# A list-scheduled attention stage, DMA transposes and a new prologue in a fused attention + token-MLP kernel

## The chip, the cores and the metric

One core of one Trainium2 chip. The metric is the device time of one execution in microseconds; the profile's span is 1 to 3 us shorter than the timed execution. TensorE does the matmuls; VectorE and ScalarE copy its results out of PSUM (the memory that matmuls write, used here as 8 banks) and do elementwise work; GpSimd does the causal masks and small operations; and SyncE issues every DMA. The program gives each engine its own list of instructions, in an order that is fixed when it is built. The kernel after was timed twice, in rounds of its own; the experiments ran in later rounds, in which the kernel before took 743.85 to 744.43 us (743.42 in the first). So a difference of under about 2 us between the kernel after and an experiment is not clear of noise, and small effects are read from the stages of the trace instead (one profiled execution each).

## The reference, cut to what matters

```python
xn = layernorm(A_x[0])                       # 2048 tokens x 1024
A: q,k,v = xn@wq, xn@wk, xn@wv               # 32 heads of 32, 4 segments of 512 tokens
   per segment: p = softmax(q k^T/sqrt(32) + causal mask);  a_dot = p v
                a_mem = phi(q) M / (phi(q) z);  o = g*a_mem + (1-g)*a_dot
                M += phi(k)^T v;  z += sum phi(k)          # phi(t) = t>0 ? t+1 : exp(t)
   a = o @ wo
B: h = layernorm(xn); u = gelu(h^T w1 + b1)  # over tokens: 2048 -> 3584 -> 2048
   y = u w2 + b2
out = A_x + a + y^T
```

`h` is the layer norm of a layer norm, so both kernels get it from one set of statistics of x.

## The kernel before

A chunk is 128 tokens (16 chunks), a unit is four heads of one segment (32 units). The kernel has four stages: prologue (loads, statistics, first hidden columns), hidden layer (896 matmuls of 128x128x512), attention with the second MLP layer between its pieces, and a tail for the last attention unit.

Prologue: statistics of a pair of chunks on VectorE, `h` on GpSimd, transposes of xn on TensorE, then six matmuls of the hidden layer per chunk:

```python
for p in range(n_pair + 2):
    if p < n_pair:
        self.ln_stats(2 * p); self.ln_stats(2 * p + 1); self.ln_small(2 * p)
    if 1 <= p <= n_pair:
        self.ln_bias(2 * p - 2)
        for c in (2 * p - 2, 2 * p - 1): self.ln_apply(c)     # xn on ACT or DVE, h on GpSimd
    # [cut]
    if p >= 2:
        for c in (2 * p - 4, 2 * p - 3):
            self.x_transpose(c)          # 8 TensorE transposes, ScalarE copies out of PSUM
            self.early_hidden(c)
```

Attention: a fixed order per unit of four heads, with fixed numbers of MLP matmuls (`main_emit`) between its pieces:

```python
self.logits(u, 0)
if u: self.combine(u - 1)
self.main_emit(n0)
self.logits(u, 1); self.main_emit(n1)
self.logits(u, 2); self.main_emit(n2)
self.weigh(u, 0); self.weigh(u, 1)
# [cut] proj_q of u+2, then
self.o_transpose(u - 1, 2)               # 4 TensorE transposes + ScalarE copy
self.k_transpose(u + 1, 3)               # 4 TensorE transposes + phi out of PSUM
self.weigh(u, 2)                         # [cut] proj_k
self.weigh(u, 3)                         # [cut] proj_v
self.main_emit(n3)
```

The softmax here doesn't subtract the row's maximum and nothing guards it: scores larger than these inputs give would overflow.

## Time and profile before

743.42 us, median of 2 runs (742.68 to 744.17). From the timeline of TensorE (start of the first hidden matmul, of the first v projection, end of the last matmul, span):

| stage | from | to | us |
|---|---|---|---|
| before the first hidden matmul | 0 | 18.9 | 18.9 |
| hidden layer | 18.9 | 223.6 | 204.7 |
| attention and output | 223.6 | 736.4 | 512.8 |
| after the last matmul | 736.4 | 742.3 | 5.9 |

Two lines of the page: the span, and busy time by engine.

```profile
span 742.3 us, 11641 instructions
...
PE 707.3 (95%) x5058; PEld 342.0 (46%) x5154; DVE 277.1 (37%) x617; ACT 280.4 (38%) x301; POOL 112.5 (15%) x154
```

The chain of waits, a part of the hidden layer: start, us, what. A piece starts every 10.79 us and holds 50 matmuls, 215.8 ns each; 49 of them are recorded, as the record of one is missing from the trace.

```profile
60.61 10.74 PE ps_all L188 x49
71.41 10.74 PE ps_all L188 x49
```

The timeline of GpSimd in the prologue gives its pace:

```profile
19.89 2.65 POOL L609 TENSOR_SCALAR h<-xin,ln_rs,ln_nb 128x1024 bf16<-128x1024 bf16 x2 [0.59 <-DVE ln_nb L594]
24.25 2.65 POOL L609 TENSOR_SCALAR h<-xin,ln_rs,ln_nb 128x1024 bf16<-128x1024 bf16 x2 [1.71 <-DVE ln_nb L594]
28.60 2.65 POOL L609 TENSOR_SCALAR h<-xin,ln_rs,ln_nb 128x1024 bf16<-128x1024 bf16 x2 [1.70 <-DVE ln_nb L594]
```

A pair of chunks of `h` comes every 4.36 us, and GpSimd waits each time for VectorE. TensorE needs 12 x 0.216 + 16 x 0.055 = 3.5 us for the same pair.

The tail, from the timeline: eight additions in four rows, each followed by its store.

```profile
732.98 3.41 PE L188 MATMUL ps_all<-wo_sb,xnT_68 128*128 128x512 bf16 x15 [0.69 <-ACT xnT_68 L835]
734.92 1.29 DVE L966 TENSOR_TENSOR fin_8027<-ps_all,fin_8027 128x512 bf16<-128x512 f32 x2 [10.19 <-PE ps_all L188]
...
738.52 1.27 DVE L966 TENSOR_TENSOR fin_8030<-ps_all,fin_8030 128x512 bf16<-128x512 f32 x2
...
739.82 0.33 SPq L210 DMA_DIRECT2D out_dram<-fin_8030  x1
```

### The profile page before, as it was taken

The numbers are of one execution on the slowest core, as the hardware profiler recorded it, in microseconds if no ns is written. First come the engines' busy times: TensorE is split into PE (matmuls) and PEld (weight loads), VectorE is DVE, ScalarE is ACT, GpSimd is POOL, SyncE is SP. The second block draws the span as 40 slices with busy tenths as digits, with TensorE's granted clock in tenths as the row PEclk, the third lists the DMA queues.
The fourth block names the chain that finished last, engine by engine and source line by source line (L and its number), as shares of the span: only waits on it lengthen the run. The fifth ranks groups of instructions, "written<-read, shape, count | busy, mean of one in ns | idle before, by whom it ended". The sixth has DMA issues, their size and how long they took to land.

```text
span 742.3 us, 11641 instructions
## 1 busy us (share of the span) xinstructions
PE 707.3 (95%) x5058; PEld 342.0 (46%) x5154; DVE 277.1 (37%) x617; ACT 280.4 (38%) x301; POOL 112.5 (15%) x154
## 2 busy tenths in 40 slices
PE   0999999999999999999999999999999999999996
PEld 0444444444444454454444455444455444444452
DVE  6930000000002234335454555554545554444543
ACT  2682121211212443544444343344444344443540
POOL 3640000000000221221121211121211112211220
PEclk9999999999999999999999999999999999999999
DMA  9429322323508141641615415052451606425003
GB/s 253 145 83 218 97 57 82 88 57 91 97 1 223 29 107 29 136 103 34 135 38 100 103 34 135 1 136 55 81 108 29 135 16 120 89 47 108 15 13 115
DMA packets 164603, 65.77 MB, mean 89 GB/s; under 512 B 125642, under 2 KB 156362, under 8 KB 164554
## 3 DMA queue, kind: packets, MB, share of 16 engines
q1 hardware_dynamic: 164554, 65.04, 37.5%
q8 instruction: 40, 0.66, 0.4%
q14 instruction: 9, 0.07, 0.0%
HBM read 59.79 MB, written 5.24 MB: 88 GB/s over the span
## 4 chain that ended last, share of the span: by engine, by line
PE 91%; DVE 4%; issue 1%; SPq 1%; ACT 1%; DMA 1%; POOL 0%; POOLq 0%; DVEq 0%
PE ps_all L188 89%; PE ps_all L194 2%; DVE ln_st L575 1%; SPq L210 1%; DVE ln_st L574 1%; DMA brow_51<-in_B_b_dram 1%; ACT pT L743 0%; DVE ln_mv L576 0%; POOL pT L749 0%; DVE xn_tmp_76 L607 0%; DVE ln_rs L584 0%; DVE fin_8030 L966 0%; DVE fin_8029 L966 0%; ACT xn_tmp_75 L604 0%; DVE xn_tmp_74 L607 0%
## 5 line engine op out<-in xcount | busy, mean ns | idle before, releaser
L743 ACT ACTIVATE pT<-ps_all 128x1536 bf16<-128x1536 f32 (+1 forms) x96 | 152.9, 1593 | 192.9 <-PE ps_all L188 192.9
L749 POOL TENSOR_SCALAR_AFFINE_SELECT pT<-pT 128x512 bf16<-128x512 bf16 x128 | 87.0, 692 | 585.1 <-ACT pT L743 585.1
L662 ACT ACTIVATE gT<-ps_all,b1c 128x512 bf16<-128x512 f32 x56 | 37.8, 689 | 134.5 <-PE ps_all L188 134.5
L710 DVE CAST vA_63<-ps_all 128x512 bf16<-128x512 f32 x16 | 11.1, 694 | 187.9 <-PE ps_all L188 187.7
L188 PE MATMUL ps_all<-h,w1s_79 128*128 128x512 bf16 x311 | 72.0, 382 | 2.7 <-issue 2.2
L188 PE MATMUL ps_all<-h,w1s_80 128*128 128x512 bf16 x314 | 72.3, 381 | 0.3
L188 PE MATMUL ps_all<-h,w1s_81 128*128 128x512 bf16 x251 | 55.6, 379 | 0.3
L188 PE MATMUL ps_all<-gT,w2h_663 128*128 128x512 bf16 x213 | 52.9, 380 | 1.1 <-issue 0.8
L188 PE MATMUL ps_all<-gT,w2h_662 128*128 128x512 bf16 x219 | 53.6, 381 | 0.3
L188 PE MATMUL ps_all<-gT,w2h_665 128*128 128x512 bf16 x214 | 53.0, 380 | 0.9 <-issue 0.6
L188 PE MATMUL ps_all<-gT,w2h_664 128*128 128x512 bf16 x218 | 53.3, 381 | 0.4 <-issue 0.2
L783 DVE CAST ost_1683<-ps_all 128x264 bf16<-128x264 f32 (+1 forms) x64 | 23.7, 391 | 71.8 <-PE ps_all L188 71.8
L783 DVE CAST ost_1684<-ps_all 128x264 bf16<-128x264 f32 (+1 forms) x64 | 23.7, 391 | 68.2 <-PE ps_all L188 68.1
L188 PEld LDWEIGHTS ps_all<-h,w1s_80 128*128 128x128 bf16 x320 | 31.4, 98 | 38.1 <-issue 0.6
L188 PEld LDWEIGHTS ps_all<-h,w1s_79 128*128 128x128 bf16 x320 | 30.7, 98 | 36.8 <-issue 3.0
L188 PEld LDWEIGHTS ps_all<-h,w1s_81 128*128 128x128 bf16 x256 | 25.0, 98 | 30.2
L188 PE MATMUL ps_all<-wo_sb,oT_1691 128*128 128x512 bf16 x126 | 32.4, 379 | 0.2
L188 PEld LDWEIGHTS ps_all<-gT,w2h_665 128*128 128x128 bf16 x224 | 20.6, 98 | 25.2 <-issue 2.5
L188 PEld LDWEIGHTS ps_all<-gT,w2h_663 128*128 128x128 bf16 x224 | 20.6, 98 | 25.2 <-issue 2.5
L188 PE MATMUL ps_all<-wo_sb,xnT_68 128*128 128x512 bf16 x127 | 30.5, 379 | 0.7 <-ACT xnT_68 L835 0.7
L188 PEld LDWEIGHTS ps_all<-gT,w2h_662 128*128 128x128 bf16 x224 | 19.3, 98 | 25.3 <-issue 6.4
L188 PEld LDWEIGHTS ps_all<-gT,w2h_664 128*128 128x128 bf16 x224 | 19.3, 98 | 25.3 <-issue 6.4
(167 smaller groups left out, 870.0 us busy)
## 6 DMA issues: line engine op xcount, KB each, us to landing
w1s_79<-in_B_w_dram SPq DMA_DIRECT2D x5, 1024.0 KB, 5.4
w1s_80<-in_B_w_dram SPq DMA_DIRECT2D x5, 1024.0 KB, 6.0
w1s_81<-in_B_w_dram SPq DMA_DIRECT2D x4, 1024.0 KB, 5.8
wq_658<-in_A_wq_dram SPq DMA_DIRECT2D x16, 256.0 KB, 3.0
wq_659<-in_A_wq_dram SPq DMA_DIRECT2D x16, 256.0 KB, 6.9
wk_660<-in_A_wk_dram SPq DMA_DIRECT2D x16, 256.0 KB, 2.9
wk_661<-in_A_wk_dram SPq DMA_DIRECT2D x16, 256.0 KB, 4.8
w2h_662<-in_B_w_dram SPq DMA_DIRECT2D x8, 448.0 KB, 4.9
```

The costliest lines, as they stand in the source:

```text
L188: ins = self.nc.tensor.matmul(*args, **kwargs)
L194: ins = self.nc.tensor.transpose(out, in_, ident)
L210: ins = es.eng.dma_start(out_ap, in_ap)
L574: fw.op("dve", lambda e: e.bn_stats(st[:, 0:6], src[:, 0:512]), reads=[self.R_xin[c]], writes=[R])
L575: fw.op("dve", lambda e: e.bn_stats(st[:, 6:12], src[:, 512:1024]), reads=[self.R_xin[c], R], writes=[R])
L662: fw.op("act", lambda e: e.activation(self.gT[:, fc, half * 512:(half + 1) * 512], self.bank(b), ACT.Gelu_apprx_tanh, bias=self.b1c[:, fc: ...
L710: fw.op("dve", lambda e: e.tensor_copy(self.vA[i][:, c, :, 0:D_HEAD], self.bank(b).rearrange("p (h d) -> p h d", d=D_HEAD)), reads=[self.R ...
L743: fw.op("act", lambda e: e.activation(self.pT[:, :, off:off + total], self.ps[:, 0:4, 0:total], ACT.Exp, scale=SCALE), reads=self.R_bank[0:4],
L749: fw.op("pool", lambda e: e.affine_select(d, d, pattern=[[0, 4], [1, P]], compare_op=ALU.is_ge, fill=0.0, base=0, channel_multiplier=-1), ...
L783: fw.op("dve", lambda e: e.tensor_copy(dst, self.ps[:, b, 0:n * VW]), reads=[self.R_bank[b]], writes=[self.R_ost[o][qb]])
```

## The change

Its intent: keep TensorE on dense matmuls from about 7 us to the end. Dense work (2816 matmuls of 512 columns) stays the same. The filler is what may be put anywhere between attention's tasks: the matmuls of the second MLP layer and of the output projection. The diff is about 1,500 lines; its core, with cuts marked:

```diff
 # --- scheduler: every operation carries an assumed duration, the builder keeps a clock per engine
+class _Flow:                       # [cut]
+    def run(self, goal, total):
+        while self.crit:           # attention's TensorE tasks, in program order
+            now = fw.now["pe"]
+            nxt = self.advance(now)          # emit ACT/DVE/POOL/SP work that is ready by now
+            # [cut] pick the first of the next 5 tasks whose inputs and PSUM banks are ready
+            ahead = fill.done >= goal * (1 - len(self.crit) / n_crit)
+            if pick is not None and (ahead or not fill.can(now)) and not (...):
+                self.emit_pe(pick); continue
+            if fill.can(now):
+                fill.step(); continue         # one dense MLP matmul
+            # [cut] else wait
+    GOAL = 1060                      # of 1088 filler matmuls
 # --- transposes: 352 on TensorE become 72 DMA transposes
-            for j in range(N_DCH):
-                fw.tp(bb[:, j * P:(j + 1) * P], src[:, j * P:(j + 1) * P], self.ident[:])
+        self.fw.dma(self.xnT[s][:, :, cc * P:(cc + 1) * P], self.xn_tmp[c % 4][:],
+                    reads=[self.R_xnt[c % 4]], writes=[self.R_xnT[c]], transpose=True)
+            # the same for k (24 of 128 KB) and o (32 of 128 KB)
 # --- logits: three windows per two units, one 512-column exponential per PSUM bank
-        fw.op("act", lambda e: e.activation(self.pT[:, :, off:off + total], self.ps[:, 0:4, 0:total], ACT.Exp, ...))
+        box = fl.pe(mms, reads, banks=len(slots), wall=True, ns=637)
 # --- prologue: x and w1 loaded by rows in turn, statistics shared with ScalarE, h on VectorE
+        self.load_x(0, 1); self.load_x(1, 1); self.load_w1(0, 1)   # [cut] x2 w1.1 x3 w1.2-3 x4-5 w1.4-5
+        fw.dma(self.brow[0:N_FCH, :], ..., reads=[self.R_brow], writes=[self.R_brow])
+        fw.dma(self.brow[32:32 + N_TCH, :], ..., reads=[], writes=[self.R_brow])
+        # [cut] x6-7 w1.6-7 ... x14-15 w1.14-15
+        self.stats(0); self.stats(1); self.ln_h(0, 0); self.ln_h(0, 1); self.stats(3)
+        for c in range(N_TCH):
+            self.early_hidden(c)                       # 8 matmuls
+            if c % 2 == 0:
+                self.stats(c + 5)                      # odd: 2 ScalarE passes, 3 GpSimd operations
+                self.stats(c + 2, 0)                   # even: VectorE, 2 GpSimd operations
+                self.ln_h(c + 1)
+                self.stats(c + 2, 1)
+                self.ln_h(c + 2)
+            if c == 10:
+                self.bias_columns()                    # 8 VectorE transposes of the bias rows
 # --- tail: stores by half, the last one by quarter
+                fw.op("dve", ..., reads=[self.R_bank[b], R_fin[i][h]], writes=[R_fin[i][h]])
+                fw.dma(self.out_d[:, 4 * s + i, h * 512 + c0:h * 512 + c1], dst, reads=[R_fin[i][h]],
+                       writes=[self.R_out[4 * s + i]], is_output=True)
```

## The prediction

> **What bounds the kernel now.** TensorE. The page gives it 95% busy; the chain of waits is 91% TensorE; the granted clock is 1.00. Dense stretches of the chain move 50 matmuls in 10.79 us, 215.8 ns each, as the Trainium skill has it ("TensorE: Matmul & The Clock Gate", Back-to-back issue gap: N/2.4 + 2.5). The 742 us, from the timeline of TensorE:
>
> - 0 to 18.8 us: no useful matmul. First x lands at 3.45; statistics wait for a 5.5 us DMA issue; TensorE sits 15.0 us on a bias row.
> - 18.8 to 225.7: hidden layer. 896 matmuls x 215.8 ns = 193.4 us, 128 transposes x 55 ns = 7.0 us, about 6.5 us of cold clock and waits.
> - 225.7 to 736.4: attention and output, 510.7 us. 1920 dense matmuls = 414.3; 1280 33-column matmuls at 25.5 ns = 32.6; 192 of 132 columns at 57 ns = 11; logits about 0.95 us x 32 = 30.5; 224 transposes x 55 ns = 12.3. Sum 501; the other 10 us are bubbles.
> - 736.4 to 742.3: eight vector additions of 0.65 us in a row, then a 2 us store.
>
> **What the change does.** The 2816 dense matmuls stay.
> - All 352 TensorE transposes go: 19.3 us of TensorE, all on the critical path. They become DMA transposes (16 of 256 KB in the hidden stage, 56 of 128 KB later). Trainium skill, "DMA: Bandwidth & Descriptors", DMA Transpose (X-bar): they run beside ordinary DMAs; no run here shows their cost. DMA is 37% busy, so I expect them hidden.
> - Prologue: loads of x and w1 interleaved by rows, half the statistics on ScalarE, h on VectorE, 14 warming matmuls, bias transposes off TensorE. Chain: x at 3.45, two statistics 1.4, aggregation 0.2, two small GpSimd operations about 0.7, half of h 0.3, hops: first hidden matmul at 6 to 8 us instead of 18.8. VectorE needs about 2.7 to 3.4 us per pair of chunks against 3.45 of TensorE: 2 to 4 us of bubbles.
> - Hidden layer ends near 7 + 193.4 + 3.5 = 204 us.
> - Attention: 488.5 us of TensorE work is left (501 less 12.3); logits in three windows per two units cost about the same. ScalarE works more (320 exponentials of about 0.6 us instead of 96 of 1.59 us, 190 us against 153) but stays half busy, VectorE too; the filler hides their latency. Bubbles 4 us (was 10): 492 us, ending at 696.
> - Tail: stores by half, last one by quarter: 3.5 us instead of 5.9.
>
> Profile span about 699.5; the times run about 1 us over the span: **701 us**, 8 in 10 between 692 and 716. Chances: faster by over 2% 0.97, within 2% 0.025, slower 0.005. In parts: prologue and its bubbles 14, x transposes 7, other transposes 12, bubbles 6, tail 2.5.
>
> **What the profile would show.** First h matmul before 8 us at 216 ns spacing; attention's first matmul at 202 to 206; no transposes on TensorE; TensorE 96 to 97% busy; attention 489 to 497 us long; DMA transposes landing in 2 to 5 us; ScalarE near 300 us busy in all; last 3 to 4 us without matmuls.
>
> **What would make it wrong.** DMA transposes that take the one issuing queue long (several us each) would delay w2 and wq loads behind them; TensorE would then wait for DMA in attention, 10 to 20 us in all. A build-time order whose assumed durations are off would stall in-order queues at the logits windows, which need six or seven free banks. A statistics chain slower than 1.73 us per chunk would stretch the early hidden stage.

## More of the kernel before

Busy time by stretch: stretch, its length, busy us (and instructions) of PE, PEld, DVE, ACT and POOL, granted clock, DMA share, GB/s.

```profile
0.00:10.00 10.00, 0.00 (x0) 0.00 (x0) 4.70 (x11) 3.00 (x4) 0.70 (x6) 1.00 0.77 186
10.00:20.00 10.00, 2.50 (x13) 1.40 (x14) 8.28 (x30) 1.56 (x4) 6.47 (x7) 1.00 1.11 340
20.00:30.00 10.00, 9.95 (x73) 5.63 (x72) 9.41 (x25) 7.72 (x10) 6.59 (x5) 1.00 0.70 211
30.00:50.00 20.00, 17.19 (x135) 9.77 (x137) 12.58 (x34) 15.29 (x19) 11.71 (x10) 1.00 0.01 2
```

TensorE does next to nothing for 18.9 us. VectorE is the busiest engine from 10 to 20 us, and from 20 to 30 us it is nearly as full as TensorE.

A small framework tracks every buffer as a `Res` with its last writer and its readers, and emits semaphore waits from that.

```python
def _waits(self, es, reads, writes, extra=()):
    # [cut] add(t): wait for token t; [cut] the rules for PSUM banks
    for r in reads:
        add(r.w)
    for r in writes:
        w = r.w
        if w is not None and isinstance(w.key, tuple) and w.key[0] == "dma" and r.r:
            pass
        else:
            add(w)                      # a second write waits for the first one
        for t in r.r.values():
            add(t)                      # and for every reader
```

## The result, and the profile after

713.83 us, median of 2 runs (713.44 to 714.21). The ratio to the kernel before is 0.9601, 95% interval 0.9573 to 0.9628. A ratio is the mean time of one kernel's fast runs over that of the other's of the same rounds, so it is not quite the ratio of the medians quoted. The prediction was 701, with 692 to 716 as its range: inside the range, and 12.8 us too low.

| stage (us) | before | after | change | predicted after |
|---|---|---|---|---|
| before the first hidden matmul | 18.9 | 6.9 | -12.0 | 7 |
| hidden layer | 204.7 | 201.6 | -3.1 | 197 |
| attention and output | 512.8 | 496.7 | -16.1 | 492 |
| after the last matmul | 5.9 | 6.6 | +0.7 | 3.5 |
| span | 742.3 | 711.7 | -30.6 | 699.5 |

The three misses are each 3 to 5 us. (The prediction put the hidden layer's end of before at 225.7; it is 223.57. I had taken the start of the view's own stretch for the start of the stage. That moved 2 us between two rows of its own account of before, and not its time for after.)

The page after:

```profile
span 711.7 us, 11510 instructions
...
PE 684.6 (96%) x4733; PEld 329.5 (46%) x4822; DVE 266.0 (37%) x600; ACT 281.6 (40%) x513; POOL 119.0 (17%) x236
```

TensorE's busy share went from 95% to 96% while the time fell by 4%, and the weight loads stayed at 46%. The Trainium skill ("Trainium Kernel Development and Optimization", Performance Expectations) calls matmul busy time a bad metric for how close a kernel is to the roofline; this agrees. The same passage calls the busy share of weight loads a good one; that did not show the gain here either, since the transposes took their weight loads with them (5154 recorded before, 4822 after).

The same stretches after:

```profile
0.00:10.00 10.00, 8.46 (x29) 3.32 (x30) 4.55 (x10) 6.21 (x11) 3.01 (x14) 1.00 0.75 236
10.00:20.00 10.00, 5.68 (x20) 2.10 (x18) 3.49 (x8) 6.93 (x13) 4.41 (x13) 0.83 0.78 271
20.00:30.00 10.00, 9.95 (x47) 4.51 (x47) 6.65 (x16) 6.41 (x12) 5.95 (x16) 1.00 0.69 229
30.00:50.00 20.00, 18.21 (x83) 7.92 (x83) 12.72 (x30) 5.65 (x10) 12.07 (x20) 1.00 0.32 97
```

From 10 to 20 us TensorE is busy for only 5.68 us, at a mean clock of 0.83, and VectorE for only 3.49 us. The timelines of TensorE, VectorE and GpSimd in that stretch (start, us, engine, what, idle before and who ended it), then of SyncE's queue:

```profile
6.85 3.61 PE L217 MATMUL ps_all<-h,w1all 128*128 128x512 bf16 x16 [0.28 <-DVE h L810]
14.78 2.59 PE L217 MATMUL ps_all<-h,w1all 128*128 128x512 bf16 x8 [4.32 <-DVE h L810]
```

```profile
8.80 0.21 DVE L798 BATCH_NORM_AGGREGATE ln_mv<-ln_st 128x2 f32<-128x12 f32 x1
14.09 0.55 DVE L810 TENSOR_SCALAR h<-xin,ln_mv,ln_r 128x1024 bf16<-128x1024 bf16 x1 [5.08 <-POOL ln_r L802]
```

```profile
9.81 0.56 POOL L789 TENSOR_TENSOR ln_r<-ln_t,mhalf 128x1 f32<-128x1 f32 x1
11.12 0.30 POOL L785 TENSOR_SCALAR ln_t<-ln_mv 128x1 f32<-128x1 f32 x1 [0.75 <-ACT xn_tmp L781]
12.28 0.19 POOL L787 TENSOR_TENSOR ln_t<-ln_t 128x1 f32<-128x1 f32 x1 [0.86 <-ACT xn_tmp L783]
12.55 0.56 POOL L789 TENSOR_TENSOR ln_r<-ln_t,mhalf 128x1 f32<-128x1 f32 x1
13.10 0.23 POOL L800 TENSOR_SCALAR ln_t<-ln_mv 128x1 f32<-128x1 f32 x1
```

```profile
5.11 5.89 SPq L245 DMA_DIRECT2D brow<-in_B_b_dram  x2
11.05 0.42 SPq L245 DMA_DIRECT2D xin<-in_A_x_dram  x1
```

Read together: chunk 2's variance is ready on VectorE at 9.0 us, but GpSimd makes its reciprocal root (L800, L802) only at 13.1, after it has done chunk 3's and chunk 5's three operations (L785 to L789). Chunk 5's wait for its load and for ScalarE. TensorE sits from 10.3 to 14.8. On SyncE, the two tiny bias rows hold the queue for 5.9 us, and no x is asked for meanwhile.

The clock then drops: the record has one window of 3.4 us at half clock from 15.8 us. The Trainium skill ("TensorE: Matmul & The Clock Gate", What's actually happening) says that an idle window of about 3.4 us brings the clock down to half. This trace agrees in the half clock and in the 3.4 us, but the 3.4 us before the drop were not idle: TensorE had been back at work for 1.0 us.

The tail, from the chain of waits after, and the end of the timeline:

```profile
702.72 0.70 DVE fin L1223
...
703.54 1.80 DMA out_dram<-fin
...
705.78 1.79 DMA out_dram<-fin
...
707.63 1.53 DMA out_dram<-fin
...
709.25 0.42 DVE fin L1223
```

Stores wait for stores in a row, and the last addition waits for a store.

The DMA transposes, from the page's list of issues (KB are not given for transposes; the last number is the median us to landing):

```profile
pk<-pkT SPq DMA_TRANSPOSE x24, 2.3
...
xnT<-xn_tmp SPq DMA_TRANSPOSE x16, 3.4
oT<-o_s SPq DMA_TRANSPOSE x16, 2.4
```

### The profile page after: what moved, and what is told of

Same layout as the page of the kernel before. It is cut to its first block, busy times and chain, and to the rows that moved or that the text cites. A ratio compares the mean times of both kernels' runs of the same rounds, so it can differ in the third digit from the quotient of the medians.

```text
span 711.7 us, 11510 instructions
## 1 busy us (share of the span) xinstructions
PE 684.6 (96%) x4733; PEld 329.5 (46%) x4822; DVE 266.0 (37%) x600; ACT 281.6 (40%) x513; POOL 119.0 (17%) x236
## 4 chain that ended last, share of the span: by engine, by line
PE 90%; DVE 3%; DMA 3%; issue 1%; ACT 1%; POOL 1%; SPq 0%; DVEq 0%
PE ps_all L217 90%; DMA xin<-in_A_x_dram 1%; DMA brow<-in_B_b_dram 1%; DVE h L810 1%; DMA w2h<-in_B_w_dram 1%; DMA out_dram<-fin 1%; DVE stg L1309 1%; DVE ln_st L796 1%; DVE ln_st L794 1%; POOL ln_r L802 0%; ACT pT L1044 0%; SPq L245 0%; DVE bt L832 0%; POOL ln_t L800 0%; DVE pkT L935 0%
## 5 line engine op out<-in xcount | busy, mean ns | idle before, releaser
L217 PE MATMUL ps_all<-gT,w2h 128*128 128x512 bf16 x850 | 219.5, 379 | 6.1 <-DVE stg L1309 2.2
L1044 ACT ACTIVATE pT<-ps_all 128x512 bf16<-128x512 f32 x320 | 162.0, 619 | 127.0 <-PE ps_all L217 127.0
L217 PE MATMUL ps_all<-h,w1all 128*128 128x512 bf16 x878 | 194.8, 381 | 7.2 <-DVE h L810 6.3
L1052 POOL TENSOR_SCALAR_AFFINE_SELECT pT<-pT 128x256 bf16<-128x256 bf16 (+3 forms) x176 | 93.5, 538 | 545.7 <-ACT pT L1044 542.0
L217 PEld LDWEIGHTS ps_all<-h,w1all 128*128 128x128 bf16 x896 | 87.7, 98 | 114.3 <-issue 9.0
L217 PEld LDWEIGHTS ps_all<-gT,w2h 128*128 128x128 bf16 x896 | 79.6, 97 | 85.3 <-issue 9.9
L217 PE MATMUL ps_all<-xnT,wq 128*128 128x512 bf16 x253 | 59.8, 379 | 2.3 <-ACT pT L1044 1.8
L217 PE MATMUL ps_all<-xnT,wk 128*128 128x512 bf16 x253 | 60.3, 379 | 0.2
L217 PE MATMUL ps_all<-wv_sb,xnT 128*128 128x512 bf16 x248 | 59.9, 379 | 0.4
L217 PE MATMUL ps_all<-vA,pT 128*128 128x33 bf16 x1280 | 51.6, 178 | 0.4
L948 ACT ACTIVATE vA<-ps_all 128x512 bf16<-128x512 f32 x18 | 10.8, 599 | 83.5 <-PE ps_all L217 83.5
```

Source lines behind the costliest of these rows:

```text
L217: ins = self.nc.tensor.matmul(out, *args, **kwargs)
L948: self.flow.op({"act": (lambda e, b: e.activation(dst, view(self.bank(b)), ACT.Copy), 635, 560), "dve": (lambda e, b: e.tensor_copy(dst, v ...
L1044: fl.op({"act": (lambda e, b, slot=slot: e.activation(pT[:, slot, :], self.bank(b), ACT.Exp, scale=SCALE), 620, 530)}, [], [R[slot]], box= ...
L1052: fl.op({"pool": (lambda e, ap=ap, pat=pat: e.affine_select(ap, ap, pattern=pat, compare_op=ALU.is_ge, fill=0.0, base=0, channel_multiplie ...
```

## The experiments

Eleven kernels were run. All gave correct results. Stage ends are read from the timeline as in the tables above.

### The two halves of the attention stage's change: before_dmat and after_pet

*before_dmat* is the kernel before with all 352 transposes made DMA transposes, with its order, prologue and tail kept (and with 110 DMA semaphores instead of 64):

```diff
 def x_transpose(self, c):
-    # 8 TensorE transposes, then a ScalarE copy
+    self.fw.dma(self.xnT[s][:, :, cc*P:(cc+1)*P], self.xn_tmp[c % 4][:], ..., transpose=True)
 def k_transpose(self, u, b):
-    # 4 TensorE transposes of kT, exp and phi from PSUM
+    # exp and phi of kT in SBUF, then
+    fw.dma(self.pk[j][:], self.etmp[1][:], ..., transpose=True)
 def o_transpose(self, u, b):
-    # 4 TensorE transposes, then a ScalarE copy
+    self.fw.dma(self.oT[s % 2][:, g, :]..., self.o_s[o][:]..., transpose=True)
```

> The kernel before with its 352 TensorE transposes made DMA transposes, nothing else (static order, old prologue, old tail). Theory A (the transposes' 19.3 us of TensorE time are wholly on the critical path, and the static order hides the DMA's 2.5 to 3.5 us as well as the list scheduler does): 722 to 726 us, attention stage 497 to 500 us. Rival B (the list scheduler is what hides the transposes' latency and the attention stage's waits): 730 us or more, with new TensorE waits on DMA.

*after_pet* is the changed kernel with the transposes of k and o put back on TensorE, as tasks of the scheduler:

```diff
-            self.flow.dma(lambda: self.fw.dma(self.pk[u % 3][:], self.pkT[:], ..., transpose=True), ...)
+            self.pe_transpose(self.pkT, self.R_pkT, pk, ...)   # 4 transposes, copy on ACT or DVE
-        t = self.flow.dma(lambda: self.fw.dma(oT[:, g, :]..., os[:]..., transpose=True), ...)
+        t = self.pe_transpose(os, R_os, oT[:, g, :], ...)
```

> The changed kernel with the 224 transposes of k and o back on TensorE, as tasks of the scheduler (evacuated by ScalarE or VectorE as it chooses); the 128 of x stay DMA transposes. Theory A (they cost TensorE 12.3 us on the critical path): 725 to 729 us, attention stage 506 to 511 us against 495 now. Rival B (the filler hides them or frees of DMA waits give half back): 718 us or less.

| | median time (4 runs if not said) | ratio to before (95%) | attention stage |
|---|---|---|---|
| before | 744.43 (7 runs) | 1 | 512.8 |
| before_dmat | 729.03 | 0.9798 (0.9781 to 0.9814) | 498.5 |
| after | 713.83 (2 runs, other rounds) | 0.9601 | 496.7 |
| after_pet | 730.88 | 0.9817 (0.9802 to 0.9831) | 513.5 |

With the old order, the DMA transposes shorten the attention stage by 14.3 us. With the scheduler, taking the k and o transposes back costs 16.8. In this stage, then, the DMA transposes are worth 14 to 17 us, and the scheduler with its new windows is worth 1.8 (498.5 against 496.7), or nothing where transposes are on TensorE (512.8 against 513.5). Even the 1.8 is not clear of noise: pool_order below has the same attention order and took 498.6. TensorE time alone would be 224 x 55 ns = 12.3 us, so after_pet lies above theory A's numbers (730.88 us, stage 513.5). Of the 2.0 us on top in before_dmat, 1.7 is the wait of TensorE in front of the first logits, which is gone. For the 4.5 us on top in after_pet no cause is shown: TensorE waits 3.6 us in front of transposes there, but less elsewhere.

As a whole before_dmat met neither of its theories' numbers (729 against 722 to 726, or 730 and more): its attention stage is as theory A had it, but its hidden stage got only 1.2 us shorter, not 7. The waits of TensorE in it, longest first, say why:

```profile
PE ps_all L194 <- DMA brow<-in_B_b_dram: 14.9, 1, 14.9
PE ps_all L188 <- POOL h L609: 5.9, 3, 2.8
```

Without the transposes TensorE waits for `h` instead. Most of the 7 us were not on the critical path of the old prologue. About 1 us more went to the DMA transposes themselves: VectorE had to wait until one had freed its buffer, and the next pair of `h` came 5.34 us after the pair before (24.34 to 29.68) instead of 4.36:

```profile
24.96 0.86 DVE L607 TENSOR_SCALAR xn_tmp<-xin,ln_rs,ln_nb 128x1024 bf16<-128x1024 bf16 x1 [0.72 <-DMA xnT<-xn_tmp]
...
29.68 2.65 POOL L609 TENSOR_SCALAR h<-xin,ln_rs,ln_nb 128x1024 bf16<-128x1024 bf16 x2 [2.80 <-DVE ln_nb L594]
```

### The tail: tail_own

```diff
-        R_fin = [[Res(...) for h in range(2)] for i in range(4)]
+        R_fin = [[Res(...) for h in range(2 + (i == 3))] for i in range(4)]   # quarters apart
-                fw.dma(..., reads=[R_fin[i][h]], writes=[self.R_out[4 * s + i]], is_output=True)
+                fw.dma(..., reads=[R_f], writes=[Res("piece")], is_output=True)
```

> The changed kernel, in which the output pieces of the tail have tracked names of their own, so that no store waits for the store before it and the last addition does not wait for its sibling's store. Theory A (these false waits are the 8 us between the last matmul and the end): 703.5 us of TensorE work stays, last addition at about 704.5 instead of 709.3, end about 3.0 us after the last matmul, time 708.5 to 709.5 us. Rival B (nine stores in a row are bound by the queue's issue, about 0.4 us each, or by the stores' own 1.7 us): the end moves by under 2 us.

709.58 us, ratio 0.9532 (0.9517 to 0.9546): 4.2 us less. From its timeline:

```profile
704.31 1.05 PE L217 MATMUL ps_all<-wo_sb,xnT 128*128 128x256 bf16 x8 [0.52 <-DVE fin L1224]
705.40 0.42 DVE L1224 TENSOR_TENSOR fin<-ps_all,fin 128x256 bf16<-128x256 f32 x1 [1.14 <-PE ps_all L217]
```

The last addition now follows its matmuls, and the span ends 2.5 us after the last matmul instead of 6.6. Theory A holds (its time was to be 708.5 to 709.5 us). The cause is one name for several pieces: both halves of an output row were tracked as one `R_out`, and both quarters of `fin` as one `Res`, so the rule "a second write waits for the first" made stores wait for stores. Each such wait costs a whole store, 1.8, 1.8 and 1.5 us above. The Trainium skill ("DMA: Bandwidth & Descriptors", Latency and other measured facts) gives about 2 us as the fixed cost of a DMA; the three agree with that roughly.

### The hole in the prologue: brow_own, pool_order, order_brow

First theory: the bias rows' false wait. Both rows are parts of `R_brow`, so the second load waits for the first to land.

```diff
-        fw.dma(self.brow[32:32 + N_TCH, :], ..., reads=[], writes=[self.R_brow])
+        fw.dma(self.brow[32:32 + N_TCH, :], ..., reads=[], writes=[self.R_brow2])
```

> The changed kernel, in which the second bias row's load no longer waits for the first one's landing (a tracked name of its own; the instruction order of all engines is the same). Theory A (the SyncE queue's 5.9 us stop at 5.1 us is this write-after-write wait, and it starves TensorE of x, 4.3 us idle, and then of its warm clock, about 2.2 us): the stop vanishes, the x chunks 4 and 5 land before 10 us, first stretch without the 4.3 us hole, granted clock 1.00 from 10 to 20 us, hidden layer ends near 202 instead of 208.4, time 707 to 708 us. Rival B (the DMA queue is full there, as the kernel before had a 5.5 us stop without such a wait): the stop only moves to the next load, and the time stays within 1.5 us of 713.8. Rival C (the statistics chain at 3.5 us per pair of chunks was the limit anyway): hole gone but the end of the early hidden stage moves by under 2 us.

712.93 us, ratio 0.9581 (0.9567 to 0.9595): a gain of about 1 us that is not clear of noise, where 6 were expected. Theory A falls. It was right about the stop, not about the hole. (The time is in rival B's range, but the stop did not just move, as B had it.) SyncE's queue and VectorE in this run:

```profile
5.11 1.87 SPq L245 DMA_DIRECT2D brow<-in_B_b_dram  x2
7.03 0.42 SPq L245 DMA_DIRECT2D xin<-in_A_x_dram  x1
```

```profile
15.02 0.55 DVE L811 TENSOR_SCALAR h<-xin,ln_mv,ln_r 128x1024 bf16<-128x1024 bf16 x1 [5.91 <-POOL ln_r L803]
```

The stop shrank from 5.9 to 1.9 us, but `h` of chunk 2 came even later, at 15.0. Chunk 5's x reached ScalarE later (10.8 against 9.9; most likely because more loads were in flight, DMA share 1.05 against 0.78 from 10 to 20 us), and chunk 2 waits for chunk 5. That pointed to GpSimd's order, which the traces above show. The Trainium skill ("PSUM — Partial Sum Buffer", Engine vs sequencer instructions) says that GpSimd's queue is strict FIFO; the trace agrees, as chunk 2's two ready operations stood behind chunk 5's. So *pool_order* only moves one emission:

```diff
             if c % 2 == 0:
-                self.stats(c + 5)
                 self.stats(c + 2, 0); self.ln_h(c + 1); self.stats(c + 2, 1); self.ln_h(c + 2)
+                self.stats(c + 5)
```

> The changed kernel with one emission moved: the ScalarE statistics of chunk c+5 are emitted after the VectorE statistics of chunk c+2 and not before them, so that GpSimd's in-order queue no longer does chunk 5's three small operations ahead of chunk 2's two. The attention stage's order is the same. Theory A (brow_own showed that chunk 2's h waits 5.9 us for GpSimd, which waits for chunk 5's load and statistics: a priority inversion, and the hole cools the clock): h of chunk 2 at about 10 us, no hole of 4 us, clock 1.00 or a little under, hidden layer ends at 202 to 204 us instead of 208.4, time 707.5 to 709.5. Rival B (the loads behind the bias row's stop at 5.1 to 11.05 us are the limit, so the hole moves to chunk 6): gain under 2.5 us. Rival C (something else holds h back): no gain.

711.59 us, ratio 0.9558 (0.9544 to 0.9572). The hidden layer ends at 205.3 instead of 208.4, and the clock stays at 1.00 in the prologue. The time gained is about half of what theory A expected, for two reasons. `h` of chunk 2 still waits 2.5 us for GpSimd, since chunk 3's operations were also ahead of it:

```profile
11.53 0.55 DVE L810 TENSOR_SCALAR h<-xin,ln_mv,ln_r 128x1024 bf16<-128x1024 bf16 x1 [2.48 <-POOL ln_r L802]
```

And the profiled execution (712.20 us, the slowest of the four) has a window of 3.4 us at half clock in the attention stage, from 337.7 us, after two waits of 0.84 and 0.79 us; its attention stage took 498.6 us, 1.9 more than that of the kernel after. *order_brow* moves those too and frees the bias row (both moves at once, so its gain over pool_order is not split):

```diff
-        self.stats(3)
         for c in range(N_TCH): ...
+                if c == 0: self.stats(3)          # after chunk 2's, before chunk 5's
```

> The changed kernel with GpSimd's statistics in the order chunk 2, chunk 3, chunk 5 (pool_order still had chunk 3's ahead of chunk 2's, and h of chunk 2 still waited 2.5 us), and the second bias row freed of its wait. Attention order unchanged. Theory A (inversion on GpSimd plus late loads are the whole hole and the cold clock; each alone only uncovers the other): h of chunk 2 at about 10 us, no hole over 0.7 us before 30 us, hidden layer ends at 201.5 to 202.5 instead of 208.4, 706.5 to 708 us. Rival (VectorE's pace of 3.5 us per pair and the bias transposes eat what is freed): hidden layer ends at 203.5 or later, 709 or more.

709.89 us, ratio 0.9548 (0.9532 to 0.9564). Chunk 2's `h` is at 10.11 us and the long hole is gone, nearly as theory A had it (TensorE's longest waits before 36 us are 0.9 to 1.1 us); but the hidden layer ends at 204.5, so the rival's number is the right one. VectorE late in the prologue shows what eats the rest:

```profile
28.68 0.55 DVE L812 TENSOR_SCALAR h<-xin,ln_mv,ln_r 128x1024 bf16<-128x1024 bf16 x1 [1.08 <-POOL ln_r L804]
29.14 1.85 DVE L834 STREAM_TRANSPOSE bt<-brow 32x32 bf16<-32x32 bf16 x8
...
31.73 0.53 DVE L812 TENSOR_SCALAR h<-xin,ln_mv,ln_r 128x1024 bf16<-128x1024 bf16 x1
```

Each pair of chunks takes VectorE 3.52 us, 1.08 of it a wait for GpSimd, and TensorE 3.45. With no slack, the 2.1 us of bias transposes (with the copy after them) are 2 us of delay: TensorE then waits 1.06 and 1.08 us for `h`.

### The filler's pace: goal900

```diff
-    GOAL = 1060
+    GOAL = 900
```

> The changed kernel with the filler paced to 900 instead of 1060 of its 1088 matmuls by the end of the attention work, so that it is spread thinner and 162 of them are left for the end. Theory A (the attention stage's 8 us of TensorE bubbles come from filler that runs out of inputs or goes ahead of its output rows, and the build-time model orders this well): the model's own stalls fall from 8.1 to 1.3 us, so 708 to 709.5 us. Rival B (the bubbles are semaphore and issue costs that no order removes): within 1.5 us of 713.8. Rival C (thin filler leaves the windows' latency open): slower than 715.

710.70 us, ratio 0.9548 (0.9533 to 0.9562): 3.1 us less, theory A in kind, but not in size (4.3 to 5.8 us less were expected). The attention stage is 493.5 us instead of 496.7. The kernel after has these waits of TensorE on ScalarE's exponentials, all between 240 and 690 us (us in total, times, longest):

```profile
PE ps_all L217 <- ACT pT L1044: 2.6, 3, 1.0
```

With GOAL = 900 they are gone, and what is left between 240 and 690 us is the filler's own:

```profile
PE ps_all L217 <- DMA w2h<-in_B_w_dram: 1.7, 2, 0.9
...
PE ps_all L217 <- DVE stg L1309: 1.0, 3, 0.4
```

The model's gain was 6.8 us of stalls; about 3 came true. Against before_dmat (498.5) the scheduler is now worth 5.0 us.

### Together: all_four, all_five, five_cold, all_six

*all_four* is tail_own, brow_own, pool_order, and the eight bias transposes split over two of VectorE's 1.1 us waits:

```diff
                     self.stats(c + 2, 1)
+                    if c in (8, 10):
+                        self.bias_columns(4 * (c // 10), 4 * (c // 10) + 4)   # 4 of 8, 0.9 us; [cut] copy after chunk 15
                     self.ln_h(c + 2)
-            if c == 10:
-                self.bias_columns()
```

> The changed kernel with the tail's stores freed of false waits, the second bias row freed of its wait, the GpSimd order of pool_order, and the eight bias transposes split over two of VectorE's 1.1 us waits for GpSimd. If the parts add: tail 4.2 us, order and bias row about 6, bias transposes 1.5 to 2: 701 to 703 us, hidden layer ends at 200 to 201.5, granted clock 1.00 throughout. If the prologue is bound by loads or by VectorE's 3.5 us per pair of chunks: 704 to 706.

704.21 us, ratio 0.9466 (0.945 to 0.9481). The time is in the range of the second expectation, so the parts do not add in full. The hidden layer ends at 202.6, and the clock is 1.00 throughout. TensorE still waits 1.7 us for chunk 2's `h`, as in pool_order.

*all_five* adds `GOAL = 900`.

> all_four with the filler paced to 900 as in goal900: the gain of goal900 on top, 696 to 698 us, if that is 5 us; the attention stage 489 to 492 us long.

700.64 us, ratio 0.9412 (0.9398 to 0.9426), another 3.6 us: slower than the expected 696 to 698 by about what goal900 alone fell short. The attention stage took 493.8 us (489 to 492 expected).

*five_cold* is all_five with `N_WARM = 1` instead of 14.

> all_five with 1 warming matmul instead of 14. If the warming pays: the first 16 hidden matmuls run at about 430 ns, clock under 1.00 before 15 us, 1.5 to 4 us more than all_five (700.6). If the hole after chunk 1 hides it: within 1 us.

700.58 us, ratio 0.942 (0.9405 to 0.9435): no difference. Its weight loads show the cold clock, one every 0.43 us, until 11.5 us:

```profile
10.64 0.15 PEld L217 LDWEIGHTS ps_all<-h,w1all 128*128 128x128 bf16 x1 [0.28 <-issue]
11.07 0.15 PEld L217 LDWEIGHTS ps_all<-h,w1all 128*128 128x128 bf16 x1 [0.28 <-issue]
11.49 4.47 PEld L217 LDWEIGHTS ps_all<-h,w1all 128*128 128x128 bf16 x21 [0.28 <-issue]
```

The cold matmuls fill the gap that TensorE would otherwise wait in for chunk 2's `h` (1.4 us in all_five). The warming matmuls buy nothing here; with the GpSimd order of all_six, which closes that gap, this was not tested.

*all_six* is all_five with the GpSimd order of order_brow, and with the first half of chunk c+4's statistics in VectorE's wait:

```diff
                     self.stats(c + 2, 1)
+                    if c and c + 4 < N_TCH: self.stats(c + 4, 0)
                     self.ln_h(c + 2)
```

> all_five with the GpSimd order of order_brow, and with VectorE's first half of the statistics of chunk c+4 put in its wait for GpSimd, so that its pace falls under TensorE's 3.45 us per pair. If both hold: hidden layer ends at 200.3 to 201 (6.9 + 193.4), 698.5 to 699.5 us. If loads bind instead: within 0.7 us of 700.6.

699.94 us, ratio 0.9408 (0.9394 to 0.9422). Its trace has the hidden layer end at 201.7 (all_five 202.4), but the ratios of the two overlap, so that it beats all_five is not shown; the time misses the expected 698.5 to 699.5 and is just inside the rival's number. A gap of 0.9 us in front of chunk 4 is left. The loads need not be its cause: GpSimd again does chunk 5's last operation (13.02 us) ahead of chunk 4's (13.56).

## Why the prediction was right or wrong

- **First hidden matmul at 6 to 8 us: right**, 6.85.
- **"2 to 4 us of bubbles" in the hidden layer: the term that failed most.** It measured 8.2 us (201.6 less 193.4). I costed VectorE's busy time per pair against TensorE's and left out the order in which GpSimd's small operations stand. The prediction's own warning, a statistics chain slower than 1.73 us per chunk, came true: 3.52 us per pair are 1.76, of which the wait for GpSimd is 0.54. The parts: 4.5 us in the hole (10.3 to 14.8), an estimated 1.7 us from one 3.4 us window at half clock, and about 2 us from bias transposes on a VectorE without slack. pool_order and order_brow show the inversion, order_brow's trace shows the bias transposes' place, and all_six leaves 1.3 us of the 8.2.
- **"All on the critical path", of all 352 transposes: half right.** For k and o it is right, and more than their 12.3 us: 14.3 (before_dmat) to 16.8 (after_pet). For x it is wrong: in the old prologue their removal gave 1.2 of 7.0 us (about 2, by estimate, without VectorE's wait for a DMA transpose). In the new prologue it was not tested. The line of the profile that said so is GpSimd's pace of 4.36 us per pair against TensorE's 3.5.
- **"Bubbles 4 us" in attention: they were 8.2** (496.7 less 488.5, which is itself the prediction's estimate of the work left). The prediction took it that list scheduling over half-idle engines would halve the bubbles. goal900 removes 3.2 us of them by pacing alone. What fixes the other 5 us was not tested.
- **"Tail 3.5 us": 6.6.** The finer stores were counted as a gain, and their tracked names were not read: the diff shows `writes=[self.R_out[4 * s + i]]` for both halves. tail_own gives 2.5 us.
- **What the change is named after** (the list scheduler) gave at most about 2 us. The DMA transposes of k and o gave about 14, the prologue 15 (12.0 and 3.1), the tail -0.7. The prediction's parts were 6 for the scheduling (the bubbles), 12 for those transposes, 21 for the prologue with the x transposes, and 2.5 for the tail. That the attention stage is only 4.7 us off is partly luck: the transposes gave more than forecast and the scheduling less.
- **DMA transposes do not choke the issuing queue: right.** They land in 2.3 to 3.4 us (medians; 6.1 at most), and in the kernel after TensorE never waits for one. The indirect wait that I named is real but small: in the chain after, one w2 load stands behind a 1.24 us transpose issue and takes 5.2 us.

Stages add up: hidden +4.6, attention +4.7 and tail +3.1 over the prediction, less 0.1 at the start, are its 12.2 us of span.

What stays open: which part of the new prologue brought the 12.0 us of earlier start (loads in turn, statistics shared with ScalarE, `h` on VectorE, bias transposes off TensorE: no run takes them apart); what the scheduler and the new logits windows did each; the split of all_four's last 2.7 us in the hidden layer (over pool_order) between the bias row and the bias transposes; and whether another order, not only another pace, would take the 5 us of attention bubbles left.

## What to carry to other kernels

A critical-path claim has to be made stage by stage: transposes were worth more than their TensorE time in one stage and about a sixth of it in another. When work is cut into finer pieces, give each piece its own name in the dependency tracking, or the pieces wait for each other; read the tracked names in the diff as closely as the operations. When one in-order engine serves several chains, even with operations of 0.2 us, emit them in the order in which their inputs come.

## What the Trainium skill lacked or had wrong

- "DMA: Bandwidth & Descriptors", DMA Transpose (X-bar): has no time for one SBUF-to-SBUF transpose of 128 or 256 KB, nor how long it holds the issuing queue (elsewhere the skill gives an effective bandwidth, and 1309 ns for one of 128x128). Here the issuing queue is held for 1.2 us per 128 KB and 1.4 us (medians) per 256 KB, where a plain 256 KB load of weights takes it 0.4 us; 128 KB land in 2.3 us and 256 KB in 3.4. The 72 of them ran among ordinary DMAs with correct results, as the page's Rules for kernel authors say.
- "TensorE: Matmul & The Clock Gate", Back-to-back issue gap: gives N/2.4 + 2.5 (215.8 ns for N = 512) as the gap of an isolated matmul only, and about 131 ns for a stream with a weight load before each matmul. The hidden layer is such a stream, and it ran at 215.8 ns.
- The same page, What's actually happening: agrees in the half-clock window (3.4 us), but the clock also fell after less than an idle window: in before_dmat after a hole of 2.8 us, in pool_order after two waits of 0.84 and 0.79 us.
- The same page does not say that a cold start can be free: 13 warming matmuls fewer changed nothing (700.58 against 700.64 us), as the cold matmuls ran in time that would have been waited out. The profile's granted clock reads 1.00 in that stretch although matmuls issue every 0.43 us, so the clock column does not show the cold start.
- "PSUM — Partial Sum Buffer", Engine vs sequencer instructions: says that the queues are FIFO, but gives no example of what it costs; here a chain of 0.8 us on GpSimd came 4 us late behind another chunk's, and pool_order took back 3.1 us of the hidden layer.
- "TensorE: Matmul & The Clock Gate", Part 4: PE-mode transpose, gives the duration of one 128x128 transpose (about 390 ns alone, 275 in one kernel), not the pace of several in a row: 55 ns each here. With the waits that hang on them, the 224 in the attention loop cost 64 ns (14.3 us) to 75 ns (16.8 us) each.
